# Input projections as seven block products in place of eight, with attention in 128-query chunks and a precomputed order

## The chip, the cores and the metric

The kernel runs on one core of a Trainium2 chip. The metric is the time of one execution on the device in microseconds (us); the kernel before takes 602.11 us, the median of three runs.

## What is computed

Causal attention over 2 batches, 12 heads, 448 positions and 64 dimensions, and then two two-layer networks on its 896 x 768 result, one behind the other, all in float32:

```
scores = q @ k.T / 8, masked above the diagonal; attn = softmax(scores)
x = (attn @ v), heads side by side                          # 896 x 768
h = x @ w_in;  g = h * clip(h + 3, 0, 6) / 6;  x = g @ w_out    # 768 -> 2048 -> 768
h = x @ w_in2; g = max(h, 0) + alpha * min(h, 0); y = g @ w_out2
```

## The kernel before

Activations are kept transposed, features on the 128 partitions and tokens along the row. 448 tokens are one block, so there are two blocks (`blk`, halves of the positions of both batches), 6 tiles of input features (`KIN`) and 16 tiles of hidden features (`KFF`). A projection is done in a split form: each float32 operand is written as a high and a low part of a reduced type (`split`, L80 on ScalarE for the high part, L81 on VectorE for the low one), and `three` (L233 to L235) multiplies high by high, high by low and low by high. Weights come as raw 64-bit words, whose conversion to float32 takes two ScalarE and two VectorE instructions of 768 columns (L207, L209, L210, L213) ahead of their split.

Attention (L89 to L180) goes over 6 pairs of heads and 2 blocks of queries, both batches each: scores (L123), a reduction on VectorE that adds the mask and finds the row maximum (L128), an exponential on ScalarE (L132), the division on GpSimd (L141), transposes on TensorE (L152) with copies out of PSUM, and the weighting of v (L165). Chunks are of 112 queries. The two heads of a pair lie on different halves of the partitions.

The input projection (`unit`, L254) forms one hidden tile of one block with 6 x 3 matmuls, applies the activation (`act1`, `act2`) and splits the result. The output projection (`outputs`, L266) forms one output tile of both blocks over all 16 hidden tiles, with weights in pieces of 5, 5 and 6 tiles. The weights' loads and conversions run some pieces ahead (`Pieces.get`). The order on each engine comes from the scheduler of the language, which sets it by a simulated time line; loads go through the queue of the Sync engine (SP), stores through ScalarE's.

Of the kernel before, what the change touches and what calls it, by code (L numbers as in the profile page):

```python
# [18 lines left out]
P = 128  # L19
CH = 112  # L20
NCH = S // CH
HALF = 2 * CH
NT = B * HALF
NBLK = 2
KIN = DM // P
KFF = DFF // P
BANK = 512
CUTS = ((0, 5), (5, 10), (10, 16))
LAST = 12
MASK = -1.0e9 * D ** 0.5  # L30
SCALE = 1.0 / D ** 0.5


def f32(t):
    return t.bitcast(F32)


class Job:


    def __init__(self, blk, c):
        self.blk, self.c = blk, c
        self.nk = 2 * (blk + 1)
        self.rows = [(i, (2 * blk + i + 1) * CH) for i in range(2)]
        self.off = [0, self.rows[0][1]]

        if blk == 0:
            self.groups = [[(0, 0, 0), (1, 1, 2 * CH)]]
        else:
            self.groups = [[(0, 0, 0), (1, 0, 2 * CH)], [(2, 0, 0), (3, 1, 2 * CH)]]  # L50


@with_exitstack
def fused_kernel(ctx: ExitStack, tc: tile.TileContext, q, k, v, w1i, w1o, w2i, w2o, alpha, out):
    nc = tc.nc
    psum = bass.MemoryType.PSUM

    const = ctx.enter_context(tc.tile_pool(name="const", bufs=1))
    xp = ctx.enter_context(tc.tile_pool(name="x", bufs=1))
    wp = ctx.enter_context(tc.tile_pool(name="w", bufs=3))  # L60
    hp = ctx.enter_context(tc.tile_pool(name="h", bufs=1))
    ps_m = ctx.enter_context(tc.tile_pool(name="ps_m", bufs=1, space=psum))

    ident = const.tile([CH, CH], F32, name="ident")
    mask = const.tile([CH, S], F32, name="mask")
    alpha_sb = const.tile([P, KFF], F32, name="alpha_sb")

    def diagonal(t, op, fill):
        nc.gpsimd.affine_select(
            out=t, in_=t, compare_op=op, fill=fill, base=0, pattern=[[-1, CH]], channel_multiplier=1  # L70
        )

    nc.gpsimd.memset(mask, 0.0)
    nc.gpsimd.memset(ident, 0.0)
    diagonal(mask[:, S - CH:S], ALU.is_ge, MASK)
    diagonal(ident, ALU.not_equal, 1.0)

    def split(hi, lo, src):

        nc.scalar.copy(hi, src)  # L80
        nc.vector.tensor_sub(lo, src, f32(hi))  # L81

    xs = {}

    def split_x(src, blk, c):
        xh = xp.tile([P, NT], F32R, tag=f"xh{blk}{c}", name="xh")
        xl = xp.tile([P, NT], F32R, tag=f"xl{blk}{c}", name="xl")
        split(xh, xl, src)
        xs[blk, c] = (xh, xl)  # L89

    def load(j):
        j.q = att.tile([P, B, HALF], F32, tag="q", name="q")
        nc.sync.dma_start(out=j.q, in_=q[j.c, :, :, j.blk * HALF:(j.blk + 1) * HALF])  # L96
        j.k = att.tile([P, B, j.nk * CH], F32, tag="k", name="k")
        nc.sync.dma_start(out=j.k, in_=k[j.c, :, :, 0:j.nk * CH])  # L98
        j.v = att.tile([CH, 2, B, j.nk, D], F32, tag="v", name="v")
        for b in range(B):  # L100
            nc.sync.dma_start(out=j.v[:, :, b], in_=v[:, 2 * j.c:2 * j.c + 2, b, 0:j.nk, :])  # L101

    def scores(j, b):
        cols = j.off[1] + j.rows[1][1]
        j.e[b] = [att.tile([CH, cols], F32, tag="e", name="e", bufs=8) for _ in range(2)]
        j.nm[b] = att.tile([CH, 2, 2], F32, tag="nm", name="nm")
        j.sm[b] = att.tile([CH, 2, 2], F32, tag="sm", name="sm")
        s = {}
        for i, n in j.rows:
            w = slice(i * CH, (i + 1) * CH)  # L110
            for side in range(2):
                if j.blk == 0 and i:
# [192 lines left out]
    n = 0  # L305
# [45 lines left out]
```

## Time and profile before

| | |
|---|---|
| runs | 600.57, 602.11, 604.17 us |
| profiled execution, span from first to last instruction | 601.3 us |
| TensorE (PE) busy | 582.3 us, 97% |
| VectorE (DVE) busy | 333.8 us, 56% |
| ScalarE (ACT) busy | 331.9 us, 55% |
| GpSimd (POOL) busy | 48.3 us, 8% |
| mean granted TensorE clock | 0.983 |

The profile is of one execution. Its span is the distance from the first to the last instruction, and the execution's own time is known only through the runs: the span stands between the fastest and the median run. Busy time of TensorE is taken from modelled ends of pipelined matmuls, so the distance from one start to the next says more than the length of a row. A fp32 matmul of attention appears as two rows. [...] A row of the time line gives start, length, engine, line, operation, output and inputs, and in brackets the idle time ahead of it with what ended it.

### The profile page before, as it was taken

What the parts mean: (1) busy time and instruction counts of PE and PEld (TensorE: products, weight loads), DVE (VectorE), ACT (ScalarE), POOL (GpSimd) and SP (SyncE); (2) the same over time, 40 slices, a digit from 0 to 9 for tenths busy, and PEclk for the clock granted to TensorE, in tenths of its full rate; (3) what the DMA queues carried; (4) which work ended last, traced back from release to release, by engine and by line L of the source; (5) the groups of instructions that cost most, each with busy time, mean ns of one, the idle gap of its engine ahead of it and who ended that gap; (6) DMA issues with size and microseconds to landing.
All of it is one profiled execution on the core that took longest, in us unless ns stands there. A gap on an engine that the chain in (4) does not pass through costs nothing.

```text
span 601.3 us, 8117 instructions
## 1 busy us (share of the span) xinstructions
PE 582.3 (97%) x3024; PEld 496.5 (83%) x3024; DVE 333.8 (56%) x632; ACT 331.9 (55%) x629; POOL 48.3 (8%) x104
## 2 busy tenths in 40 slices
PE   5799999889999999999999999999999999999997
PEld 2355555469999999999999999999999999999996
DVE  3566665855777755754444454777776654344310
ACT  4566775845755655643443445887777754334210
POOL 2334445030000000000000000000000000000000
PEclk9889999789999999999999999999999999999999
DMA  8523334413333322343323433333323333453000
GB/s 235 168 64 88 114 93 136 158 53 105 106 106 105 102 93 87 100 137 121 116 88 106 158 106 105 106 106 105 106 87 100 128 105 119 126 156 112 32 32 31
DMA packets 23224, 64.63 MB, mean 108 GB/s; under 512 B 2192, under 2 KB 13712, under 8 KB 23184
## 3 DMA queue, kind: packets, MB, share of 16 engines
q1 hardware_dynamic: 21456, 61.36, 32.5%
q10 hardware_dynamic: 1728, 2.75, 1.2%
q8 instruction: 24, 0.39, 0.3%
q14 instruction: 16, 0.13, 0.1%
HBM read 61.35 MB, written 2.75 MB: 107 GB/s over the span
## 4 chain that ended last, share of the span: by engine, by line
PE 93%; DMA 3%; SPq 1%; ACT 1%; DVE 1%; issue 0%; ACTq 0%
PE m L234 26%; PE m L233 26%; PE m L235 26%; PE o L165 6%; PE t L152 5%; PE s L123 4%; DMA raw<-w1i 2%; DMA k<-k_t 1%; SPq L101 0%; DVE raw L210 0%; ACT wf L207 0%; SPq L96 0%; SPq L98 0%; ACT raw L209 0%; DVE e L128 0%
## 5 line engine op out<-in xcount | busy, mean ns | idle before, releaser
L233 PE MATMUL m<-xh,hi 128*128 128x448 f32 x384 | 141.5, 368 | 2.7 <-ACT xh L80 2.7
L234 PE MATMUL m<-xl,hi 128*128 128x448 f32 x384 | 140.9, 367 | 0.0
L233 PE MATMUL m<-gh,hi 128*128 128x448 f32 x384 | 140.2, 365 | 0.0
L235 PE MATMUL m<-gh,lo 128*128 128x448 f32 x384 | 140.2, 365 | 0.0
L234 PE MATMUL m<-gl,hi 128*128 128x448 f32 x384 | 140.2, 365 | 0.0
L235 PE MATMUL m<-xh,lo 128*128 128x448 f32 x384 | 140.2, 365 | 0.0
L81 DVE TENSOR_TENSOR lo<-wf,hi 128x768 fp32r<-128x768 f32 (+1 forms) x68 | 61.9, 911 | 96.2 <-ACT hi L80 95.2
L80 ACT CAST hi<-wf 128x768 fp32r<-128x768 f32 (+1 forms) x68 | 54.2, 797 | 89.9 <-PE m L234 89.8
L210 DVE SCALAR_TENSOR_TENSOR raw<-wf,raw 128x768 uint32<-128x768 uint32 (+1 forms) x68 | 62.1, 913 | 67.7 <-ACT wf L207 58.0
L233 PEld LDWEIGHTS m<-xh,hi 128*128 128x128 f32 x384 | 72.3, 188 | 10.0 <-ACT xh L80 2.9
L234 PEld LDWEIGHTS m<-xl,hi 128*128 128x128 f32 x384 | 72.1, 188 | 7.0 <-issue 1.0
L209 ACT ACTIVATE raw<-raw 128x768 uint32<-128x768 uint32 (+1 forms) x68 | 59.3, 873 | 32.9 <-DMA raw<-w1o 13.2
L235 PEld LDWEIGHTS m<-gh,lo 128*128 128x128 f32 x384 | 72.1, 188 | 5.7
L233 PEld LDWEIGHTS m<-gh,hi 128*128 128x128 f32 x384 | 72.1, 188 | 5.7
L234 PEld LDWEIGHTS m<-gl,hi 128*128 128x128 f32 x384 | 72.1, 188 | 5.7
L235 PEld LDWEIGHTS m<-xh,lo 128*128 128x128 f32 x384 | 72.1, 188 | 5.6
L207 ACT ACTIVATE wf<-raw 128x768 f32<-128x768 f32 (+1 forms) x68 | 57.9, 851 | 30.4 <-DVE lo L81 22.4
L213 DVE SCALAR_TENSOR_TENSOR wf<-wf,raw 128x768 uint32<-128x768 uint32 (+1 forms) x68 | 61.8, 909 | 1.5
L132 ACT ACTIVATE e<-e,nm 112x112 f32<-112x112 f32 (+2 forms) x96 | 50.0, 523 | 20.5 <-DVE nm L128 16.1
L80 ACT CAST gh<-hg 128x448 fp32r<-128x448 f32 x64 | 36.0, 562 | 38.3 <-DVE hg L243 21.7
L141 POOL TENSOR_SCALAR e<-e,r 112x112 f32<-112x112 f32 (+1 forms) x96 | 47.0, 507 | 78.9 <-DVE r L137 64.2
L123 PE MATMUL s<-k,q 64*112 64x112 f32 (+3 forms) x192 | 42.9, 500 | 10.7 <-DMA k<-k_t 4.9
(32 smaller groups left out, 425.8 us busy)
## 6 DMA issues: line engine op xcount, KB each, us to landing
raw<-w1i SPq DMA_DIRECT2D x16, 768.0 KB, 4.4
raw<-w2i SPq DMA_DIRECT2D x16, 768.0 KB, 4.2
raw<-w1o SPq DMA_DIRECT2D x12, 640.0 KB, 4.0
raw<-w2o SPq DMA_DIRECT2D x12, 640.0 KB, 4.1
raw<-w1o SPq DMA_DIRECT2D x6, 768.0 KB, 4.3
raw<-w2o SPq DMA_DIRECT2D x6, 768.0 KB, 4.3
q<-q_t SPq DMA_DIRECT2D x12, 224.0 KB, 3.5
k<-k_t SPq DMA_DIRECT2D x6, 448.0 KB, 3.7
```

The lines of the kernel that those rows point to most:

```text
L80: nc.scalar.copy(hi, src)
L81: nc.vector.tensor_sub(lo, src, f32(hi))
L123: nc.tensor.matmul(s[i, side], lhsT=j.q[d, b, w], rhs=j.k[d, b, 0:n], start=True, stop=True)
L132: nc.scalar.activation(e, e, AF.Exp, bias=nm, scale=-1.0, accum_out=sm)
L141: nc.gpsimd.tensor_scalar(e, e, r[:, side, i:i + 1], 1.0, ALU.mult, ALU.mult)
L207: nc.scalar.activation(f32(w), f32(high), AF.Copy, scale=2.0 ** -112)
L209: nc.scalar.activation(low, low, AF.Copy, bias=-0.4999, scale=2.0 ** -29 * (1 - 2.0 ** -16))
L210: nc.vector.scalar_tensor_tensor(out=low, in0=w, scalar=3, in1=low, op0=ALU.logical_shift_left, op1=ALU.bitwise_or)
L213: nc.vector.scalar_tensor_tensor(out=w, in0=w, scalar=0x80000000, in1=low, op0=ALU.bitwise_and, op1=ALU.bitwise_or)
L233: nc.tensor.matmul(ps, lhsT=hi[:, w], rhs=xh, start=start, stop=False)
L234: nc.tensor.matmul(ps, lhsT=hi[:, w], rhs=xl, start=False, stop=False)
L235: nc.tensor.matmul(ps, lhsT=lo[:, w], rhs=xh, start=False, stop=stop)
```

## The change

**Input projection.** Strassen's scheme replaces the plain product. Hidden tiles m and m + 8 form a pair, the input features are cut in two halves of three tiles, and the tokens are the two blocks, each now one batch: a 2 x 2 by 2 x 2 product of blocks with seven products (`w_in`, named by b11, t1, t2, b22, t3, b21, t4) in place of eight. Each product is 3 tiles x 3 matmuls. The sums of x (t1 to t4) are formed and split once per tile in `take_x`; the sums of the weights (s12, s34) are formed on VectorE for every pair, and all three 768-column sets and one of 384 columns are split. PSUM banks a and c keep running sums: they are read between two products (`kept`), and the next product adds to the same bank (`again=not start`). What is read is added up in SBUF tiles on VectorE (`add_to`), then the activation follows (`finish`).

**Output projection.** Three output tiles of both blocks at a time (six banks), in two passes over the hidden tiles. The high and low parts of the hidden tiles are made in the first pass.

**Attention.** Twelve units (head pair, batch) with query chunks of 128, 128, 128 and 64; in the last chunk both heads share one matmul of 128 rows. Transposed blocks are packed into four banks per unit. Keys and queries of a unit come in one load.

**Order.** A program written in the kernel (`Plan.solve`) puts every instruction on its engine at build time, from costs given with it, due times and numbers of buffers. Stores go through SP's queue.

The core of the diff:

```diff
...
-    def three(ps, hi, lo, i, xh, xl, start, stop):
-        w = slice(i * P, (i + 1) * P)
-        nc.tensor.matmul(ps, lhsT=hi[:, w], rhs=xh, start=start, stop=False)
-        nc.tensor.matmul(ps, lhsT=hi[:, w], rhs=xl, start=False, stop=False)
-        nc.tensor.matmul(ps, lhsT=lo[:, w], rhs=xh, start=False, stop=stop)
...
-    def unit(pool, layer, blk, m, hi, lo):
-
-        ps = pool.tile([P, NT], F32, tag="m", name="m")
-        for kk in range(KIN):
-            three(ps, hi, lo, kk, *xs[blk, kk], kk == 0, kk == KIN - 1)
-        g = act2(ps, m) if layer else act1(ps)
-        gpool = gp["first"] if (blk, m) == (0, 0) else gp["last"] if m >= LAST else gp["main"]
-        gh = gpool.tile([P, NT], F32R, tag=f"gh{blk}_{m}", name="gh")
-        gl = gpool.tile([P, NT], F32R, tag=f"gl{blk}_{m}", name="gl")
-        split(gh, gl, g)
-        gs[blk, m] = (gh, gl)
-
-    def outputs(pool, n, done):
-
-        for c in range(KIN):
-            tiles = [pool.tile([P, NT], F32, tag="m", name="m") for _ in range(NBLK)]
-            for k0, k1 in CUTS:
-                hi, lo = pieces.get(n)
-                n += 1
-                for blk in range(NBLK):
-                    for kk in range(k0, k1):
-                        three(tiles[blk], hi, lo, kk - k0, *gs[blk, kk], kk == 0, kk == KFF - 1)
-                    if k1 == KFF:
-                        done(tiles[blk], blk, c)
-        return n
...
+                    if ok:
+                        key = (round(t, 2), o.due, o.index)
+                        if best is None or key < best[0]:
+                            best = (key, e, o, t)
...
+        return sorted(done, key=lambda o: (o.start, o.index))
...
+    def take_x(self, layer, c, blk, ps):
+
+        j, low = c % HK, c < HK
+        x, f = self.x, self.f
+        src, n = (lambda: ps.tile[:, 0:S]), f"{layer}{j}"
+
+        def parts(which, t):
+            x[layer, which, j] = self.split("u", which + n, S, lambda: t.tile, t)
+
+        if low and blk:
+            f["b12", j] = Buf("u", "b12" + n, S, F32)
+            self.copy(f["b12", j], src, ps, S)
+        elif low:
+            x[layer, "b11", j] = self.split("u", "b11" + n, S, src, ps)
+            b12 = f["b12", j]
+            f["t1", j] = self.combine("t1" + n, lambda: b12.tile, src, b12, ps)
+            parts("t1", f["t1", j])
+        elif blk:
+            x[layer, "b22", j] = self.split("u", "b22" + n, S, src, ps)
+            b12, t1 = f["b12", j], f["t1", j]
+            f["t2", j] = self.combine("t2" + n, src, lambda: t1.tile, ps, t1)
+            t3 = self.combine("t3" + n, src, lambda: b12.tile, ps, b12)
+            parts("t2", f["t2", j])
+            parts("t3", t3)
...
+            x[layer, "b21", j] = self.split("u", "b21" + n, S, src, ps)
+            t2 = f["t2", j]
+            parts("t4", self.combine("t4" + n, src, lambda: t2.tile, ps, t2))
...
+    def three(self, ps, hi, lo, at, x, start, stop, due, again=False):
+
+        nc, (xh, xl) = self.nc, x
+
+        def emit(_):
+            w, out = slice(at, at + P), ps.tile[:, 0:S]
+            for lhs, rhs in ((hi, xh), (hi, xl), (lo, xh)):
+                nc.tensor.matmul(
+                    out, lhsT=lhs.tile[:, w], rhs=rhs.tile, start=start and lhs is hi and rhs is xh,
+                    stop=stop and lhs is lo, skip_group_check=again)
+
+        self.cols += 1
+        return self.plan.op((PE, 0.605), emit, reads=[hi, lo, xh, xl], writes=[ps], due=due + self.cols * 0.605, chain="moe")
...
+    def w_in(self, layer, m, src, due):
+        nc, op = self.nc, self.plan.op
+        w1, w2 = self.convert(src[m]), self.convert(src[m + PAIRS])
+        s12, s34 = Buf("w", "s12", DM, F32), Buf("w", "s34", DM, F32)
...
+        add, sub = nc.vector.tensor_add, nc.vector.tensor_sub
+        sums(s12, right, w2, left, w2, right, add, [w2])
+        sums(s12, left, s12, right, w1, left, sub, [(s12, W3), w1])
+        sums(s34, right, w1, right, s12, left, sub, [w1, (s12, 0)])
+        sums(s34, left, w1, left, w2, left, sub, [w1, w2])
...
+        p12 = both("a1", DM, lambda: f32(w1.tile), [w1])
+        p56 = both("s12", DM, lambda: s12.tile, [(s12, 0), (s12, W3)])
+        p37 = both("s34", DM, lambda: s34.tile, [(s34, 0), (s34, W3)])
+        p4 = both("a2", W3, lambda: f32(w2.tile[:, right]), [w2])
...
+        def product(ps, parts, at, which, start):
+            for kk in range(HK):
+                o = self.three(ps, *parts, at + kk * P, self.x[layer, which, kk], start and kk == 0,
+                               kk == HK - 1, due, again=not start)
+            return o.due
...
+        product(a, p12, 0, "b11", True)
+        g11 = kept("g11", a)
+        product(c, p56, W3, "t1", True)
+        g22 = kept("g22", c)
+        product(a, p56, 0, "t2", False)
+        g12 = kept("g12", a)
+        end = product(c, p37, W3, "b22", False)
+        add_to(g12, c)
+        finish(g12, m, 1, end + 5.0)
+        end = product(a, p37, 0, "t3", False)
+        add_to(g22, a)
+        finish(g22, m + PAIRS, 1, end + 5.0)
+        end = product(b, p12, W3, "b21", True)
+        add_to(g11, b)
+        finish(g11, m, 0, end + 5.0)
+        end = product(a, p4, 0, "t4", False)
+        g21 = Buf("u", "g21", S, F32)
+        finish(g21, m + PAIRS, 0, end + 4.0, ps=a)
+
+    def w_out(self, layer, src, due, done):
+        halves = {}
+        for h in range(2):
+            banks = {(j, blk): Buf("ps", f"y{j}{blk}") for j in range(HK) for blk in range(2)}
+            for k0 in range(0, PAIRS, 2):
+                parts = []
+                for kp in (k0, k0 + 1):
+                    w = self.convert(src[h, kp])
+                    parts.append(self.split("w", "wo", DM, lambda w=w: f32(w.tile), w))
+                order = [(j, blk) for j in range(HK) for blk in (1, 0)]
+                if h == 0 and k0 == 0:
+                    order = [(j, blk) for blk in (1, 0) for j in range(HK)]
+                for j, blk in order:
+                    for i, kp in enumerate((k0, k0 + 1)):
+                        for kk, k in enumerate((kp, kp + PAIRS)):
+                            if h == 0 and (k, blk) not in halves:
+                                g = self.g[k, blk]
+                                halves[k, blk] = self.split("u", f"g{k}{blk}", S, lambda g=g: g.tile, g)
+                            o = self.three(banks[j, blk], *parts[i], kk * W3 + j * P, halves[k, blk], k == 0,
+                                           k0 == PAIRS - 2 and i == 1 and kk == 1, due)
+                    if k0 == PAIRS - 2:
+                        done(layer + 1, HK * h + j, blk, banks[j, blk])
...
+    def build(self):
+        nc, op, d = self.nc, self.plan.op, self.dram
+        start, step = 9.0, 6.2
+        for n in range(2 * KIN):
+            self.attend(n, n // 2, 1 - n % 2, start + (n + 1) * step)
...
+        due = start + 2 * KIN * step - 2.0
+        for layer, (w_in, w_out) in enumerate((("w1i", "w1o"), ("w2i", "w2o"))):
+            for m in range(PAIRS):
+                self.w_in(layer, m, d[w_in], due)
+            self.w_out(layer, d[w_out], due, self.take_x if layer == 0 else self.store)
...
+SLOTS = {"u": 50, "w": 14, "raw": 3, "kq": 2, "v": 3, "e": 12, "el": 3, "small": 6, "a": 2, "ps": 8, "alpha": 1}
...
+            o.emit(o.eng)
...
```

How the order of the instructions stands on the engines, at three places. VectorE, one hidden tile of both blocks in layer 0 before (L243 activation, L81 low parts, L210 and L213 conversion):

```order
L243 SCALAR_TENSOR_TENSOR hg<-hr,m 128x448
L81 TENSOR_TENSOR gl<-hg,gh 128x448
L210 SCALAR_TENSOR_TENSOR raw<-wf,raw 128x768
L243 SCALAR_TENSOR_TENSOR hg<-hr,m 128x448
L213 SCALAR_TENSOR_TENSOR wf<-wf,raw 128x768
L210 SCALAR_TENSOR_TENSOR raw<-wf,raw 128x768
L81 TENSOR_TENSOR gl<-hg,gh 128x448
```

Each activation is followed by the low part of its result, with the conversion of later weights between them. VectorE in the changed kernel, part of one pair of hidden tiles in layer 0 (L209 and L212 conversion, L418 sums of weights, L430 their low parts, L457 additions out of PSUM, L466 activation):

```order
L212 SCALAR_TENSOR_TENSOR wf<-wf,raw 128x768
L418 TENSOR_TENSOR s_1491<-wf 128x384
L430 TENSOR_TENSOR a1l<-wf,a1h 128x768
L418 TENSOR_TENSOR s_1491<-s_1491,wf 128x384
L457 TENSOR_TENSOR g_1489<-c,g_1489 128x448
L418 TENSOR_TENSOR s_1513<-wf,s_1491 128x384
L430 TENSOR_TENSOR s12l<-s_1491,s12h 128x768
L457 TENSOR_TENSOR g_1471<-a,g_1471 128x448
L466 SCALAR_TENSOR_TENSOR g_1489<-r,g_1489 128x448
```

The sums of weights and the additions out of PSUM are new, and the low parts of the hidden tiles no longer stand there.

TensorE in the changed kernel, where the second unit's weighting ends and the third and fourth units' scores begin (L387 weighting, L297 the last chunk's scores, L291 those of the others):

```order
L387 MATMUL o<-a,v 64x448 x2
L387 MATMUL o<-a,v 64x320 x2
L297 MATMUL sl<-kq 128x448
L387 MATMUL o<-a,v 64x192 x2
L291 MATMUL s_293<-kq 128x384
L291 MATMUL s_294<-kq 128x384
L387 MATMUL o<-a,v 64x64 x2
L291 MATMUL s_303<-kq 128x256
L291 MATMUL s_304<-kq 128x256
```

The scores of two units now stand together, ahead of the transposes of the first of them; before, the scores of part of a unit alternated with transposes and weighting.

## Rows read from the trace of the kernel before

**Rows 1.** The page's first part: busy time, share of the span, instructions.

```profile
span 601.3 us, 8117 instructions
PE 582.3 (97%) x3024; PEld 496.5 (83%) x3024; DVE 333.8 (56%) x632; ACT 331.9 (55%) x629; POOL 48.3 (8%) x104
```

**Rows 2.** Busy time by stretch of the span; the first line names the columns.

```profile
core 0: us, PE busy (x) PEld busy (x) DVE busy (x) ACT busy (x) POOL busy (x), PEclk, DMA share, GB/s
...
20.00:39.62 19.62, 15.74 (x80) 8.56 (x78) 11.93 (x44) 12.82 (x39) 6.11 (x14) 0.74 0.22 69
39.62:57.04 17.42, 17.42 (x126) 9.92 (x125) 12.42 (x51) 12.32 (x41) 7.02 (x16) 1.00 0.37 107
...
109.30:133.40 24.10, 22.25 (x141) 13.57 (x141) 17.55 (x39) 14.88 (x35) 5.51 (x8) 0.85 0.31 99
133.40:597.80 464.40, 464.36 (x2296) 429.90 (x2292) 253.19 (x331) 247.71 (x375) 0.00 (x0) 1.00 0.32 103
```

**Rows 3.** Time line of TensorE, end of the last output projection: 54 steps apart.

```profile
586.04 0.36 PE L233 MATMUL m<-gh,hi 128*128 128x448 f32 x1
...
596.98 0.37 PE L233 MATMUL m<-gh,hi 128*128 128x448 f32 x1
```

**Rows 4.** Time line of all engines behind the last matmul.

```profile
597.39 0.37 PE L235 MATMUL m<-gh,lo 128*128 128x448 f32 x1
597.80 0.53 ACT L282 COPY o<-m 128x448 f32<-128x448 f32 x1 [3.12 <-PE m L235]
598.36 0.34 ACTq L283 DMA_DIRECT2D y_t<-o  x1
```

**Rows 5.** Time line of VectorE in attention, 70 to 72 us.

```profile
70.00 0.50 DVE L128 CUSTOM_DVE_ANT_0 e<-s,mask 112x336 f32<-112x336 f32 x1
...
70.42 0.62 DVE L128 CUSTOM_DVE_ANT_0 e<-s,mask 112x448 f32<-112x448 f32 x1
...
70.96 0.62 DVE L81 TENSOR_TENSOR xl<-o,xh 128x448 fp32r<-128x448 f32 x1
71.50 0.49 DVE L128 CUSTOM_DVE_ANT_0 e<-s,mask 112x336 f32<-112x336 f32 x1
```

**Rows 6.** Time line of VectorE in the first input projection.

```profile
150.51 0.96 DVE L210 SCALAR_TENSOR_TENSOR raw<-wf,raw 128x768 uint32<-128x768 uint32 x1 [2.23 <-ACT wf L207]
...
151.51 0.96 DVE L213 SCALAR_TENSOR_TENSOR wf<-wf,raw 128x768 uint32<-128x768 uint32 x1
...
152.39 0.62 DVE L81 TENSOR_TENSOR gl<-hg,gh 128x448 fp32r<-128x448 f32 x1
```

**Rows 7.** Groups by line and shape, ScalarE: busy us, mean ns of one.

```profile
L209 ACT ACTIVATE raw<-raw 128x768 uint32<-128x768 uint32 x44 | 40.3, 916 | 18.5 <-DMA raw<-w2i 5.5 <-DMA raw<-w1i 5.3 <-DMA raw<-w1o 4.5
...
L242 ACT ACTIVATE hr<-m 128x448 f32<-128x448 f32 x32 | 17.2, 539 | 7.4 <-PE m L235 7.4
```

**Rows 8.** Time line of TensorE in attention, 56 to 75 us.

```profile
56.98 1.01 PE L123 MATMUL s<-k,q 64*112 64x448 f32 x4
57.92 0.59 PE L152 MATMUL t<-ident,e 112*112 112x112 f32 x4
58.44 0.59 PE L165 MATMUL o<-a,v 112*64 112x224 f32 x2
...
72.31 1.55 PE L165 MATMUL o<-a,v 112*64 112x224 f32 x16
73.79 0.47 PE L234 MATMUL m<-xl,hi 128*128 128x448 f32 x1
```

**Rows 9.** Time line of ScalarE in attention.

```profile
58.69 0.67 ACT L132 ACTIVATE e<-e,nm 112x448 f32<-112x448 f32 x1 [1.42 <-DVE nm L128]
...
59.35 0.85 ACT L154 COPY a<-t 112x448 f32<-112x448 f32 x2
...
65.99 0.38 ACT L132 ACTIVATE e<-e,nm 112x112 f32<-112x112 f32 x1
...
66.36 0.47 ACT L132 ACTIVATE e<-e,nm 112x224 f32<-112x224 f32 x1
```

**Rows 10.** Time line of TensorE, its first matmuls.

```profile
4.89 2.59 PE L123 MATMUL s<-k,q 64*112 64x112 f32 x16 [4.89 <-DMA k<-k_t]
```

**Rows 11.** Waits of the whole span: total us, times, longest.

```profile
DVE lo L81 <- ACT hi L80: 95.2, 50, 6.6
```

More of the change, by code (lines that the diff above doesn't have):

```diff
@@ L7 @@
 from concourse import mybir
-from concourse.bass import opposite_side
 from concourse._compat import with_exitstack
@@ L35, in f32, with __init__ @@
     return t.bitcast(F32)
[L38 to L48, printed above, removed]
-        else:
-            self.groups = [[(0, 0, 0), (1, 0, 2 * CH)], [(2, 0, 0), (3, 1, 2 * CH)]]
+class Buf:
+    def __init__(self, cls, name, cols=None, dtype=None):
+        self.cls, self.name, self.cols, self.dtype = cls, name, cols, dtype
+        self.left, self.end, self.slot, self.tile = 0, 0.0, None, None
@@ L68, in diagonal @@
     def diagonal(t, op, fill):
         nc.gpsimd.affine_select(
[L70 to L89, printed above, removed]
@@ L94, in load @@
[L94 to L112, printed above, removed]
-                    s[i, side] = bank[side][:, j.off[1]:j.off[1] + n]
-                else:
-                    t = ps_s.tile([CH, BANK], F32, tag="s", name="s")
-                    s[i, side] = t[:, 0:n]
-                    if side == 0:
-                        bank = [t]
-                    else:
-                        bank.append(t)
-            for side in range(2):
-                d = slice(side * D, (side + 1) * D)
-                nc.tensor.matmul(s[i, side], lhsT=j.q[d, b, w], rhs=j.k[d, b, 0:n], start=True, stop=True)
-        for i, n in j.rows:
-            for side in range(2):
-                e = j.e[b][side][:, j.off[i]:j.off[i] + n]
-                nm, sm = j.nm[b][:, side, i:i + 1], j.sm[b][:, side, i:i + 1]
-                nc.vector.tensor_tensor_reduce(
-                    out=e, in0=s[i, side], in1=mask[:, S - n:S], scale=-SCALE, scalar=3.0e38,
-                    op0=ALU.add, op1=ALU.min, accum_out=nm,
-                )
-                nc.scalar.activation(e, e, AF.Exp, bias=nm, scale=-1.0, accum_out=sm)
@@ L304, in fused_kernel @@
-    gp["last"] = ctx.enter_context(tc.tile_pool(name="g_last", bufs=1, reuse_waits="tile"))
-    n = 0
-    for layer, done in enumerate((split_x, store)):
-        for m in range(KFF):
-            if layer or m:
-                parts = pieces.get(n)
-                for blk in range(NBLK):
-                    unit(ps, layer, blk, m, *parts)
-            n += 1
-        n = outputs(ps, n, done)
+            out=t, in_=t, compare_op=op, fill=fill, base=0, pattern=[[-1, P]], channel_multiplier=1)
@@ L320 @@
     c = np.ascontiguousarray
[L321 to L339 removed]
+    cuts = ((3 * P, S), (2 * P, 3 * P), (P, 2 * P), (0, P))
@@ new lines @@
+    y = r.results[0]["y_t"].reshape(DM, B, S)
+    out = np.empty((B, S, DM), np.float32)
+    at = 0
+    for lo, hi in cuts:
+        out[:, lo:hi] = y[:, :, at:at + hi - lo].transpose(1, 2, 0)
+        at += hi - lo
+    return out.reshape(B * S, DM)
```

542 lines of the change are left out of this document (384 added, 158 removed), and 4 rows, old and new, of the table banks.

## The prediction

> **What bounds the kernel now.** I read the page's busy times first, then the table of stretches, then the matmul rows at the end, and last the attention rows of each engine. TensorE is busy 97% of the span, VectorE 56%, ScalarE 55% [rows 1]. The table of stretches splits the span in two [rows 2]. [...] Before 133.4 us the kernel computes attention, and there all engines matter: in a steady period of 17.42 us (one of the six head pairs) TensorE is shown busy throughout, VectorE 12.42 us, ScalarE 12.32 us. At the end of the span matmuls start every 0.2026 us: from 586.04 to 596.98 us lie 54 steps [rows 3]. So the 2304 projection matmuls cost 2304 x 0.2026 = 466.8 us. The last ends near 597.75 us, which leaves 130.9 us ahead of or between them, and 3.5 us of copy and store behind [rows 4]. The sum is made against the profiled span of 601.3 us; the median of the runs is 602.1, 0.8 above it, and I add that at the end.
>
> **Projection matmuls.** Per pair of hidden blocks the input projection has 7 products of 9 matmuls, 63, where it had 72. Sixteen pairs save 144 of 2304; 2160 are left, as the changed order's rows also count. At 0.2026 us that is 29.2 us off, if nothing else becomes late. Of the 2160, 24 stand among the attention rows, so 2136 x 0.2026 = 432.8 us remain behind it. The output projection keeps its 1152 matmuls; the order of accumulation alone changes.
>
> **What Strassen puts on VectorE.** A VectorE step is the distance from one start to the next where nothing waits. A 336-column reduction takes 0.42 us, a 448-column one 0.54, a 448-column subtraction 0.54 [rows 5]. A 768-column step is 0.88 us where the next instruction does not read its result (L213 to the gl row), and 1.00 where it does (L210 to L213) [rows 6]. The new 384-column sums have no row: between 0.42 and 0.54, I take 0.47, the value on the line through 448 and 768 columns. Per pair: four bit operations 4 x 0.88 = 3.5; four sums 1.9; three low parts of 768 and one of 384 columns 3.1; three additions out of PSUM and four activations 7 x 0.54 = 3.8. That is 12.3 us; 13 of the 48 PSUM copies stand on VectorE, 0.15 more, and one or two steps per pair read the row before them, 0.12 each. About 12.6 us against TensorE's 63 x 0.2026 = 12.76: VectorE goes from 55% to 99% of TensorE's time in this stage. The cover is gone, so anything that makes VectorE late now reaches TensorE. With 15 pairs behind the attention I allow 4 us, between 0 and 8. ScalarE has at most 4 bit operations, 3.5 splits, 4 activations and 2.2 copies, under 10.5 us even at 0.92 for each 768-column one and 0.54 for each of 448 [rows 7], and stays out of it. The splits of the 32 hidden tiles of each layer are moved behind the last pair, among the output matmuls: the rows from pair 7's last activation to pair 8's hold 90 us of VectorE work beside 192 x 0.608 + 12.8 = 129 us of matmuls, so they cost nothing; without that cover they would add 32 x 0.54 = 17 us a layer. At the seam of the layers I put 1 us.
>
> **Attention.** A fp32 matmul is here two rows in the trace, and the two sides of a head pair run side by side. The 448-column pair takes 0.94 us from 56.98 to 57.92, four transposes 0.52 us, and the weighting of 784 columns (both sides together) 1.48 us from 72.31 to 73.79 [rows 8]. That is 0.0021 us a score column, 0.13 a transpose of 112 (0.149 for 128 columns in proportion), 0.0019 a weighting column. Old, per period: 2240 score columns 4.7, 40 transposes 5.2, 2240 weighting columns 4.2, 3 projection matmuls 0.6: 14.7 of 17.42 us, so 84% is work and the rest hand-offs. New, per unit (head pair, batch): 128 + 256 + 384 + 448 = 1216 score columns 2.55, 16 transposes 2.38, 448 + 320 + 192 + 64 = 1024 weighting columns 1.93: 6.86 us. Twelve units are 82.3, with the 24 projection matmuls 87.2 us. Of the transposes 36 write two 64-column pieces; no row shows such a store. Between no change and twice the price it is 0 to 5 us; I take 0, the price of the transposes that do have rows. VectorE's rows up to TensorE's last weighting come to 78 us: 84 reductions at 0.08 + 0.00103 per column, 31; 23 copies of 512 columns at 0.61, 14; 27 splits and combinations of x, 14.5; the first weights, 14; the rest 4. ScalarE has about 77: an exponential of 448 columns steps 0.66 us and one of 112 columns 0.37 [rows 9], so 84 take 44, copies 12, splits and weights 21. GpSimd's 40 us are hidden as before. TensorE first ran at 4.89 us, released by a load [rows 10]; the new first load, 480 KB by the code, is about as large as the q and k that it replaces, so 4.9 stands. The stage then ends no earlier than 4.9 + 87.2 = 92 us (no hand-off ever waits), and 4.9 + 87.2/0.845 = 108 if the share of work stays as it was. I take 102, nearer 108, because three engines now have 77 to 87 us in the same stage, where VectorE and ScalarE had 71%; less than 108 because the old stage also lost time in 20 to 39.6 and in 109.3 to 133.4 us [rows 2], where weights were late, and the new order has their loads spread among the units'. 1 us is for the last splits of x.
>
> **Moved queues.** Stores go from ScalarE's queue to SP's, behind the weight loads; the last load is long done at the end, so the tail keeps its 3.5 us. Conversions of weights fall from 68 to 64.
>
> **Sum.** 102 + 1 + 432.8 + 4 + 1 + 3.5 = 544.3 us against 601.3: 29 us off from the matmuls, 28 from attention and its seam. With 0.8 for the median, 545.
>
> **Rivals.**
> *VectorE bounds the input projections.* If each of its 20 instructions per pair cost its whole duration (0.96 instead of 0.88, 0.62 instead of 0.54 [rows 5, 6]), a pair would take 12.3 + 20 x 0.08 = 13.9 us, 1.15 over TensorE; 15 pairs are 17 us in place of the 4: 558, up to 564 with a late attention. For it: VectorE already waits 95 us in all for ScalarE's high parts [rows 11], and each such wait is now paid. Against it: rows 5 and 6 show the next instruction starting 0.08 before the end of the last. [...]
> *The clock falls in attention.* [...] If the new stage, with VectorE and ScalarE as full as TensorE, ran at 0.80 throughout, TensorE's 87.2 us would become 109: 566.
> *Slower than before: the shared accumulator.* Banks a and c now hold sums that are read between two products and added to again. Four times per pair TensorE must not write on until the reader has finished, and only one other product, 9 x 0.2026 = 1.82 us, lies between. The read takes about 0.54, so a reader that starts more than 1.2 us after the product stops TensorE. With 64 such places, a mean stop of 0.9 us gives 58 us back: 602 and above. For it: the readers stand in the queue of a VectorE with 0.88 us steps ahead of them. Against it: ScalarE took 35 of the copies, and the last copy of the old kernel started at 597.80, about 0.05 us after its matmul [rows 4].
> *Attention packs tightly* and VectorE keeps up: 92 + 432.8 + 4.5 = 529 or less.
>
> **How the numbers follow.** The forecast (529 to 556) gets 0.70, VectorE as bound 0.13, the clock 0.08, the accumulator 0.04, less than 529 0.04; 0.01 is left for no change, since the order shows that the matmuls are in fact fewer. A difference of over 0.5% is what a measurement can tell. Range: 92 + 0.5 + 432.8 + 0 + 0.5 + 3.5 = 529 below; above, the VectorE case with attention ending at 108, 564. Faster 0.95, same 0.01, slower 0.04.
>
> **What would show it.** Right: about 2160 matmul rows of 448 columns starting every 0.2026 us; the last attention matmul near 102 us; VectorE over 90% busy in the input projections and TensorE still over 95%. Wrong: TensorE rows idle behind VectorE's low parts (the first rival), a granted clock under 0.9 before 100 us (the second), idle TensorE in front of products into a or c, released by a copy or an addition (the third), or an attention stage that ends outside 92 to 108 us.

## The result, and the profile after

The changed kernel takes **549.59 us** (median of 4 runs, 548.38 to 553.24) where the kernel before takes 603.14 (4 runs beside it): a ratio of 0.911, 95% interval 0.907 to 0.916. The profiled execution took 548.4 us with a span of 546.6; the forecast was 545 and a span of 544.3. The total is 0.8% off, but two groups of its terms are off by more, in opposite directions.

Busy time of the engines, from the page of the kernel after, to be read beside [rows 1]:

```profile
PE 528.2 (97%) x2712; PEld 459.8 (84%) x2712; DVE 428.0 (78%) x773; ACT 337.9 (62%) x627; POOL 53.5 (10%) x97
```

The table of stretches of the kernel after, beside [rows 2]: time, then busy time and instruction count of PE, PEld, DVE, ACT and POOL, TensorE's granted clock, DMA share, GB/s. The first line is the attention stage, the next two lie inside it, the fourth is the input projection of layer 0 behind the attention, the last that of layer 1.

```profile
4.20:109.34 105.14, 94.63 (x576) 58.86 (x576) 87.33 (x268) 81.07 (x230) 50.98 (x84) 0.94 0.38 132
26.10:40.00 13.90, 10.14 (x51) 6.59 (x51) 11.23 (x39) 11.09 (x35) 6.82 (x10) 0.75 0.39 132
60.00:80.00 20.00, 20.00 (x139) 11.69 (x138) 18.65 (x66) 16.73 (x53) 12.59 (x23) 1.00 0.38 115
109.34:206.00 96.66, 96.66 (x481) 89.60 (x478) 95.22 (x149) 71.56 (x115) 0.00 (x0) 1.00 0.33 115
322.00:425.00 103.00, 102.94 (x508) 94.76 (x507) 102.38 (x159) 75.38 (x121) 0.00 (x0) 1.00 0.35 121
```

In both input projections VectorE is busy 98 to 99% of the time, and TensorE hardly stops (102.94 of 103.00 us busy in layer 1). In the attention it is the other way round: TensorE is idle 105.14 - 94.63 = 10.5 us, all of it before 57 us, and from 26.10 to 40.00 us the granted clock falls to 0.75.

TensorE's time line at the seam, where the first projection matmul behind the attention follows the last weighting, and at the end of the span, with VectorE's last copy (beside [rows 3, 4]):

```profile
109.34 0.47 PE L404 MATMUL a<-t202h,s12h 128*128 128x448 f32 x1
...
542.62 0.36 PE L404 MATMUL y<-g150h,wol 128*128 128x448 f32 x1
543.01 0.62 DVE L230 COPY o<-y 128x448 f32<-128x448 f32 x1 [1.80 <-PE y L404]
```

From 109.34 to 543.01, where the last copy starts, lie 433.7 us; 2136 matmuls at 0.2026 are 432.8. The whole projection stage lost 0.9 us. The tail is 546.6 - 543.0 = 3.6 us.

VectorE's time line inside layer 0's input projection shows the steps that the forecast had to assume ([rows 5, 6]):

```profile
156.51 0.95 DVE L209 SCALAR_TENSOR_TENSOR raw<-wf,raw 128x768 uint32<-128x768 uint32 x1
157.38 0.62 DVE L466 SCALAR_TENSOR_TENSOR g<-g,a 128x448 f32<-128x448 f32 x1
157.91 0.62 DVE L230 COPY g<-a 128x448 f32<-128x448 f32 x1
...
160.18 0.55 DVE L430 TENSOR_TENSOR a2l<-wf,a2h 128x384 fp32r<-128x384 f32 x1
160.65 0.95 DVE L212 SCALAR_TENSOR_TENSOR wf<-wf,raw 128x768 uint32<-128x768 uint32 x1
```

A 768-column step is 0.87 us, a 448-column one 0.53, a 384-column one 0.47.

What is new stands in the attention. GpSimd's time line, three of twelve units (x6 joins the divisions of the first 384 query rows of both sides, two each of 384, 256 and 128 columns), and under it VectorE's over the second of these stretches:

```profile
12.60 2.75 POOL L338 TENSOR_SCALAR e<-e,small 128x384 f32<-128x384 f32 x6
...
38.92 5.35 POOL L338 TENSOR_SCALAR e<-e,small 128x384 f32<-128x384 f32 x6
...
79.94 2.75 POOL L338 TENSOR_SCALAR e<-e,small 128x384 f32<-128x384 f32 x6
```

```profile
39.42 0.95 DVE L430 TENSOR_TENSOR s12l<-s,s12h 128x768 fp32r<-128x768 f32 x1
40.28 0.62 DVE L222 TENSOR_TENSOR t100l<-t,t100h 128x448 fp32r<-128x448 f32 x1
40.82 0.62 DVE L318 CUSTOM_DVE_ANT_0 el<-sl,mask 128x448 f32<-128x448 f32 x1
41.36 0.08 DVE L318 DVE_READ_ACCUMULATOR2_ANT small<- 128x1 f32 x1
41.36 1.17 DVE L430 TENSOR_TENSOR s34l<-s,s34h 128x768 fp32r<-128x768 f32 x1
...
42.99 1.04 DVE L209 SCALAR_TENSOR_TENSOR raw<-wf,raw 128x768 uint32<-128x768 uint32 x1
```

The same six divisions take 2.75 us in some units and up to 5.35 in others. Meanwhile VectorE runs four instructions that read two SBUF tensors, and the two of 1.17 and 1.04 us are longer than their usual 0.95 us as well. TensorE's waits in the first 109 us (total, times, longest) name who is late:

```profile
PE t L353 <- POOL e L338: 4.9, 8, 1.2
PE t L345 <- POOL el L338: 1.4, 1, 1.4
PE a L404 <- DVE b1101l L222: 2.1, 1, 2.1
PE a L404 <- DVE b1100l L222: 2.1, 1, 2.1
```

PE's lines make up the 10.5 us of idle time: 6.3 behind divisions, and 4.2 behind something else. Among the attention stand the first matmuls of the projection; two of them stand in TensorE's order before the low part of x that they read is ready: VectorE made it only after reductions of later units. The first of the two, with the matmul before it:

```profile
29.68 0.47 PE L404 MATMUL a<-b1100h,a1h 128*128 128x448 f32 x1
32.26 0.55 PE L404 MATMUL a<-b1100l,a1h 128*128 128x448 f32 x1 [2.11 <-DVE b1100l L222]
```

### The profile page after: what moved, and what is told of

Its sections match the earlier page's. It is cut to its first block, busy times and chain, and to the rows that moved or that the text cites. A ratio compares the mean times of both kernels' runs of the same rounds, so it can differ in the third digit from the quotient of the medians.

```text
span 546.6 us, 7448 instructions
## 1 busy us (share of the span) xinstructions
PE 528.2 (97%) x2712; PEld 459.8 (84%) x2712; DVE 428.0 (78%) x773; ACT 337.9 (62%) x627; POOL 53.5 (10%) x97
## 3 DMA queue, kind: packets, MB, share of 16 engines
HBM read 59.38 MB, written 2.75 MB: 114 GB/s over the span
## 4 chain that ended last, share of the span: by engine, by line
PE 91%; DVE 3%; POOL 3%; ACT 1%; issue 1%; DMA 1%; POOLq 0%; DVEq 0%
PE y L404 42%; PE a L404 20%; PE c L404 10%; PE b L404 5%; PE o L387 5%; PE t L353 3%; PE s L291 3%; POOL e L338 3%; PE sl L297 2%; PE t L345 1%; DMA kq<-kq 1%; ACT e L323 1%; DVE e L318 1%; DVE t L239 0%; POOL el L338 0%
## 5 line engine op out<-in xcount | busy, mean ns | idle before, releaser
L207 ACT ACTIVATE raw<-raw 128x768 uint32<-128x768 uint32 x64 | 58.8, 919 | 40.6 <-DMA raw<-w2i 18.8
L205 ACT ACTIVATE wf<-raw 128x768 f32<-128x768 f32 x64 | 57.1, 903 | 16.1 <-PE y L404 13.5
L209 DVE SCALAR_TENSOR_TENSOR raw<-wf,raw 128x768 uint32<-128x768 uint32 x64 | 61.5, 962 | 2.6 <-ACT wf L205 2.6
L212 DVE SCALAR_TENSOR_TENSOR wf<-wf,raw 128x768 uint32<-128x768 uint32 x64 | 61.2, 957 | 1.5
L222 DVE TENSOR_TENSOR wol<-wf,woh 128x768 fp32r<-128x768 f32 x32 | 30.4, 953 | 21.4 <-PE y L404 17.3
L338 POOL TENSOR_SCALAR e<-e,small 128x384 f32<-128x384 f32 (+2 forms) x72 | 43.6, 628 | 0.0
L221 ACT CAST woh<-wf 128x768 fp32r<-128x768 f32 x32 | 26.3, 836 | 21.1 <-PE y L404 13.6
L323 ACT ACTIVATE e<-e,small 128x384 f32<-128x384 f32 (+2 forms) x72 | 35.7, 501 | 2.9 <-DVE small L318 2.7
L318 DVE CUSTOM_DVE_ANT_0 e<-s,mask 128x384 f32<-128x384 f32 (+2 forms) x72 | 26.7, 417 | 2.5 <-PE s L291 1.8
L387 PE MATMUL o<-a,v 128*64 128x448 f32 (+3 forms) x192 | 28.2, 401 | 0.0
L387 PEld LDWEIGHTS o<-a,v 128*64 128x64 f32 (+1 forms) x192 | 13.4, 137 | 17.3 <-issue 10.2
L430 DVE TENSOR_TENSOR s12l<-s,s12h 128x768 fp32r<-128x768 f32 x16 | 15.2, 951 | 12.4 <-PE y L404 12.4
L418 DVE TENSOR_TENSOR s<-wf 128x384 f32<-128x384 f32 x32 | 17.8, 555 | 8.3 <-PE y L404 7.7
L291 PE MATMUL s<-kq 64*128 64x384 f32 (+2 forms) x144 | 22.3, 426 | 0.0
L291 PEld LDWEIGHTS s<-kq 64*128 64x128 f32 x144 | 13.0, 197 | 9.9 <-issue 5.6
```

Source lines behind the costliest of these rows:

```text
L205: op((ACT, 0.85), lambda e: nc.scalar.activation(f32(w.tile), f32(words(1)), AF.Copy, scale=2.0 ** -112), reads=[(raw, "h")], writes=[w])
L207: op((ACT, 0.87), lambda e: nc.scalar.activation(words(0), words(0), AF.Copy, bias=-0.4999, scale=2.0 ** -29 * (1 - 2.0 ** -16)), writes=[ ...
L209: op((DVE, 0.87), lambda e: nc.vector.scalar_tensor_tensor(out=words(0), in0=w.tile, scalar=3, in1=words(0), op0=ALU.logical_shift_left, o ...
L212: op((DVE, 0.87), lambda e: nc.vector.scalar_tensor_tensor(out=w.tile, in0=w.tile, scalar=0x80000000, in1=words(0), op0=ALU.bitwise_and, o ...
L222: op((DVE, 0.14 + 0.00094 * cols), lambda e: nc.vector.tensor_sub(lo.tile, src(), f32(hi.tile)), reads=[key, hi], writes=[lo])
L291: nc.tensor.matmul(t.tile[:, off:off + (i + 1) * P], lhsT=kq.tile[rows, S + i * P:S + (i + 1) * P], rhs=kq.tile[rows, 0:(i + 1) * P], star ...
```

## Experiments

Experiments 1 to 4, 8 and 9 are one execution each. Experiment 4 leaves the attention as it is and ends it at 108.56 us against 109.34, so differences of under 1 us there say nothing.

**Theory:** attention ends 7.3 us later than forecast because the weights' new VectorE work holds GpSimd's divisions, and TensorE's transposes wait for them. **Rival:** TensorE's own rows and its lower clock set the end, and GpSimd is hidden. For the projections, the theory is that VectorE has almost nothing to spare; the rival is that its busy time overstates its load. The end of attention is read in each run as the start of the first projection matmul behind the last weighting (109.34 above).

**1. No divisions.** The seven GpSimd divisions of each unit emit nothing.

```diff
-            op((POOL, ...), lambda _, ...: nc.gpsimd.tensor_scalar(...),
+            op((POOL, ...), lambda _, ...: None,
```

> The 84 divisions on GpSimd (the softmax rows times the reciprocal of their sum, L338) are left out, so the attention output is not normalised; the order of every other instruction stays. Theory (divisions stand in the chain exponential - division - transpose, and 17 of them are lengthened while VectorE works on two SBUF inputs): the last weighting ends near 100 us instead of 109.3 and the span falls by 7 to 10 us, to about 538. Rival (TensorE's own rows and its lower clock before 40 us set the end of attention, GpSimd is hidden): the last weighting ends at 107 us or later and the span stays above 544.

Measured: span 540.5, end of attention 103.19.

```profile
3.91:103.13 99.22, 91.97 (x576) 58.98 (x576) 82.92 (x268) 80.31 (x230) 0.00 (x0) 0.95 0.42 140
```

The span falls 6.1 us, all of it in the attention: less than the theory's 7 to 10, but more than the rival allows. VectorE's busy time falls by 4.4 us too, with the same 268 instructions: it had been slowed by the divisions. TensorE is still idle 99.22 - 91.97 = 7.2 us, 4.1 of them before the two matmuls that wait for x's low parts. This run removes a whole step of the chain, so it does not yet show that the *meeting* costs the time.

**2. One input.** In the first two pairs of layer 0 each VectorE step on the weights that reads two SBUF tensors becomes one of the same columns on a single tensor.

```diff
+        def lone(out, src):
+            nc.vector.reduce_max(out.unsqueeze(2), src.unsqueeze(2), axis=mybir.AxisListType.X)
...
-            op((DVE, ...), lambda _: nc.vector.tensor_sub(lo.tile[:, 0:cols], src(), f32(hi.tile[:, 0:cols])),
+            op((DVE, ...), lambda _: lone(lo.tile[:, 0:cols], src()) if one else nc.vector.tensor_sub(...),
```

> In the first two pairs of layer 0 the bit operations, sums and low parts of the weights on VectorE (L209, L212, L418, L430) are replaced by instructions of the same columns that read one SBUF tensor only, so the products of these two pairs have other values; order and number of instructions stay. Theory (a GpSimd division is held while VectorE reads two SBUF tensors): the lengthened divisions before 80 us fall from 13 to about 4, their excess from 8.2 to under 2.5 us, and the last weighting ends 3 to 7 us earlier, near 104 us. Rival 1 (the long divisions are a symptom, GpSimd simply takes turns): as many lengthened divisions as before and no gain. Rival 2 (they are held, but nothing waits for them): the divisions get short and the last weighting still ends within 1 us of 109.3.

Measured: end of attention 102.64, 6.7 us earlier, with every division still there. GpSimd's groups (busy, mean ns), first of the kernel after, then of this run:

```profile
L338 POOL TENSOR_SCALAR e<-e,small 128x256 f32<-128x256 f32 x24 | 16.9, 717 | 0.0
L338 POOL TENSOR_SCALAR e<-e,small 128x384 f32<-128x384 f32 x24 | 16.9, 716 | 0.0
```

```profile
L341 POOL TENSOR_SCALAR e<-e,small 128x384 f32<-128x384 f32 x24 | 15.0, 637 | 0.0
L341 POOL TENSOR_SCALAR e<-e,small 128x256 f32<-128x256 f32 x24 | 12.3, 526 | 0.0
```

The 256-column divisions fall from 717 to 526 ns; after the change they had been as slow as those of 384 columns. The replacements last as long as what they replace (groups of 941 to 944 ns at 768 columns against 950 where the original meets no division), so VectorE's own load is the same and only the kind of its reads differs. The wait of TensorE's transposes for these divisions falls from 4.9 us to

```profile
PE t L356 <- POOL e L341: 1.2, 3, 0.7
```

while those for x's low parts stay (2.1 and 2.2 us). In the stretch from 26.10 to 40.00 TensorE now has

```profile
26.10:40.00 13.90, 11.56 (x69) 7.90 (x70) 12.92 (x43) 12.84 (x37) 6.93 (x14) 0.88 0.41 134
```

69 instructions instead of 51, at a clock of 0.88 instead of 0.75. The theory holds: both rivals fall. The clock rises as the waits shrink (over the attention from 0.94 to 0.97, TensorE's idle time from 10.5 to 6.9 us), although the edit is on VectorE alone. Not separated is whose delay counted: the edit frees the divisions, and it also takes 2.6 us of lengthening off VectorE (84.75 us busy for 87.33). The span falls by 3.4 us only, to 543.2: 0.9 us went in layer 1's input projection and 2.3 in its output projection, where from 366 us on the matmuls start 0.2067 us apart instead of 0.2026 (last section).

**3. Strassen undone.** 8 plain block products per pair; scheduler, attention and output passes kept.

```diff
-        a, b, c = Buf("ps", "a"), Buf("ps", "b"), Buf("ps", "c")
...
+        self.x[layer, c, blk] = self.split("u", f"x{layer}{c}{blk}", S, lambda: ps.tile[:, 0:S], ps)
```

> Strassen alone is undone: 8 block products of 9 matmuls per pair, no sums on VectorE, the same list scheduling, attention and output passes. Theory (the matmul count is what the stage costs, VectorE's additions cost it nothing there): 2304 matmuls at 0.2026 us, the projection stage 29 us longer than 434, 462 to 464 us; the attention stage ends 3 to 8 us earlier than 109.3 because VectorE and GpSimd no longer meet there; span 568 to 573. Rival (a part of the gain is the accumulation in place and the two output passes, or VectorE's work did cost TensorE time): the projection stage is under 458 us and the span under 565.

Measured: span 573.3. The attention stage and the stretch behind it:

```profile
4.13:104.30 100.17, 90.92 (x567) 55.69 (x567) 79.47 (x251) 80.52 (x224) 48.51 (x84) 0.95 0.48 162
104.30:215.00 110.70, 109.88 (x544) 101.51 (x541) 75.72 (x103) 64.43 (x102) 0.00 (x0) 1.00 0.32 107
```

Weighting ends 5.0 us earlier, as expected, and the projections stay at the pitch of 0.2026; the span is 0.3 us above what was expected. So Strassen is worth 573.3 - 546.6 = 26.7 us here: 144 matmuls, 29.2, and 1.8 for nine more matmuls that find room inside the attention (24 against 15), less the 5.0 us by which the weighting ends later with it; the 0.7 left over is a wait in this run, whose first projection matmul starts 0.85 us after the last weighting instead of 0.15. The expectation's reason for the 5.0, that VectorE and GpSimd no longer meet, is not borne out: GpSimd is busy 48.51 us for 50.98, and 10 divisions are still longer than others of their width, by 8.0 us in all (17 and about 10.5 us in the changed kernel), since the bit operations and low parts remain. What clearly falls is VectorE's work, 79.47 us for 87.33. The other 28.0 us of the change (601.3 to 573.3) came without Strassen, nearly all in the attention; what the larger chunks, the packed transposes and the new order each gave was not tried.

**4. One more low part.** 0.87 us more VectorE work in each of 14 pairs.

```diff
+            twice = name == "a1" and not (layer == 0 and m < 2)
...
+                for _ in range(1 + twice):
+                    nc.vector.tensor_sub(lo.tile[:, 0:cols], src(), f32(hi.tile[:, 0:cols]))
```

> In all pairs but the first two of layer 0 one 768-column low part (L430) is computed twice: 0.87 us more VectorE work per pair, 14 pairs, values unchanged. Theory (VectorE has 0.2 us of slack per pair of 12.76 us, 95.2 us busy of 96.7 in the first layer's pairs, so it is the next bound): TensorE waits 0.6 us per pair, 4 us in the first layer and 4 to 5 in the second, span 554 to 556. Rival (busy time overstates the load, or the weights prepared ahead cover it): the span grows by less than 2 us.

Measured: span 557.3. Layer 0's and layer 1's input projections:

```profile
108.50:210.30 101.80, 99.40 (x484) 89.62 (x481) 100.84 (x155) 71.23 (x116) 0.00 (x0) 1.00 0.32 109
327.20:436.60 109.40, 104.28 (x505) 93.82 (x504) 108.54 (x166) 74.59 (x121) 0.00 (x0) 1.00 0.33 109
```

From first to last matmul, layer 0 loses 4.65 us over 0.2026 a matmul (0.14 before) and layer 1 7.5 (0.5 before): 0.75 a pair in layer 0, where 0.12 was spare, and all 0.87 in layer 1. The theory was right and still too mild for layer 1, where no slack is left. Where TensorE then waits is of interest too, in layer 1:

```profile
PE a L404 <- DVE g L462: 5.1, 7, 1.3
```

L462 is the addition out of an accumulator that the next product needs.

**5 to 7. Buffers and order.** One kernel gets a third key-and-query buffer for one buffer of `u`; one gets the trace's costs and held divisions in the scheduler's model; one gets both.

```diff
-SLOTS = {"u": 50, ..., "kq": 2, ...}
+SLOTS = {"u": 49, ..., "kq": 3, ...}
```

```diff
-        op((PE, 0.24), score(0), ...)
+        op((PE, 0.42), score(0), ...)
...
+            if e == POOL:
+                if lock > t:
+                    o.out = o.end = clock[e] = o.end + lock - t
+                held = o
+            if e == DVE and o.two:
+                lock = o.end
+                if held is not None and held.end > t:
+                    held.out = held.end = clock[POOL] = held.end + o.end - t
```

> One more buffer for the scaled keys and queries of a unit (3 in place of 2), paid with one buffer of u; everything else is left to the scheduler with its old costs. Theory (TensorE idles before 40 us because the divisions of two units are late and it has no third unit's scores to compute meanwhile): the last weighting starts 3 to 7 us before 109.2 and the time falls by as much, to 543 to 547. Rival (the divisions and VectorE set the pace of the whole stage, however many units are open): within 1.5 us of 109.2.

> The same kernel, with the scheduler's costs of scores, weightings and ScalarE steps set to those of the trace, and a GpSimd division held in its model while VectorE has an instruction on two SBUF tensors; buffers unchanged. Theory (the order was made for divisions that are never held, so units whose division is late stand ahead of others in TensorE's queue): the excess of the divisions falls from 10.5 us to under 6 and the last weighting starts 2 to 5 us before 109.2. Rival (any order meets the same divisions, total work sets the end): within 1.5 us of it.

> Both: the trace's costs with the held divisions in the scheduler's model, and the third buffer of keys and queries. Theory: the gains add, the last weighting starts at 98 to 103 us and the time is 539 to 543. Rival (the two reach the same idle time): no better than the better of the two alone, within 1 us. In the projections nothing may move by over 2 us in either case, since TensorE runs there at 0.2026 us a matmul.

Measured against 602.95 us before (7 runs): third buffer **543.60** (ratio 0.902, 0.897 to 0.906), new costs **542.25** (0.901, 0.895 to 0.906), both **537.36** (0.894, 0.888 to 0.900; of its four runs three took 537.3 and one 543.39). The attention stages in this order:

```profile
4.15:101.55 97.40, 91.49 (x576) 55.98 (x576) 83.28 (x266) 78.29 (x227) 49.12 (x84) 0.98 0.41 137
```

```profile
4.20:106.40 102.20, 95.51 (x594) 62.69 (x594) 88.74 (x274) 84.19 (x237) 48.60 (x84) 0.98 0.41 136
```

```profile
4.00:97.15 93.15, 90.81 (x576) 59.41 (x576) 83.66 (x268) 80.02 (x231) 49.98 (x84) 1.00 0.44 150
```

The third buffer ends the stage 7.8 us earlier, a little more than expected; the new order 2.9 us, and it places 18 more matmuls (3.6 us) in the stage besides; the two together 12.1 us, more than expected. With both, TensorE is busy 90.81 of 93.15 us at full clock. But GpSimd is busy 49.12, 48.60 and 49.98 us, hardly less than the 50.98 of the change: the gain is not that divisions are held less, as the second expectation had it. The waits of TensorE tell more. Those for x's low parts, 4.2 us, are gone in all three, as the projection matmuls come later in its order. Those of the transposes for divisions were 4.9 us after the change; with the third buffer, and then with both, they are

```profile
PE t L353 <- POOL e L338: 5.0, 5, 1.8
PE t L366 <- POOL e L351: 0.3, 1, 0.3
```

So the third buffer alone leaves TensorE waiting for divisions as before. Only with the new order as well does TensorE have other units' work meanwhile. This version beats both kernels, and it is the one to keep.

**8. The same replacement in that kernel.** The diff of experiment 2, on the kernel with both.

> The replanned kernel with three key buffers, and in the first two pairs of layer 0 the VectorE steps on two SBUF tensors replaced by ones on a single tensor (the products of these pairs have other values); same order. Theory (what holds the last weighting at 97.1, 5 us over TensorE's own 92, is again mostly held divisions, whose excess is 9.2 us): the excess falls under 3 us and the last weighting starts at 93 to 95. Rival (with a third unit open TensorE has other work while a division is held): at 96.5 or later. The span then follows by at most as much, since VectorE has less than 0.2 us a pair to spare in the projections.

Measured: end of attention 96.09 against 97.21.

```profile
3.90:96.05 92.15, 89.61 (x576) 58.50 (x576) 81.93 (x268) 79.43 (x231) 42.63 (x84) 1.00 0.45 152
```

GpSimd's busy time falls by 7.35 us and the stage by 1.1: between the two expectations, nearer the rival. A held division costs little with a third unit open and the new order. The span rose to 541.4, which the last section explains.

**9. The meeting by itself.** Ahead of the attention GpSimd multiplies in a row while VectorE runs six blocks of ten.

```diff
+        for _ in range(60):
+            nc.gpsimd.tensor_scalar(gt, gt, gs, 1.0, ALU.mult, ALU.mult)
...
+        for f in (bank, one, both, bank, copy, both):
+            for _ in range(10):
+                f()
```

> The cost of the meeting by itself: ahead of the attention GpSimd multiplies a 256-column tile 60 times in a row, while VectorE, not waiting for it, runs six blocks of ten 448-column instructions: PSUM and SBUF in, one SBUF tensor in (the instruction of the run before), two SBUF tensors in, PSUM and SBUF again, a plain SBUF copy, two SBUF tensors again. Theory (GpSimd is held for the whole of each VectorE instruction that reads two SBUF tensors): GpSimd's instructions take 485 ns beside the first, second and fourth block, and over 1000 ns, or hardly any ends, beside the third and sixth; VectorE's own take up to 0.15 us longer where they meet. No theory for the copy. Rival (the two share bandwidth, no one is held): everything beside the third block is longer by the same modest share, under a third. The main part's time is not read from this run.

Measured, from the time line of GpSimd and VectorE around the second block, and then around the third:

```profile
9.45 6.76 POOL L595 TENSOR_SCALAR gt<-gt,gs 128x256 f32<-128x256 f32 x12
9.49 6.51 DVE L596 TENSOR_REDUCE zt<-xt 128x448 f32<-128x448 f32 x10
```

```profile
15.73 8.64 POOL L595 TENSOR_SCALAR gt<-gt,gs 128x256 f32<-128x256 f32 x11
16.03 8.00 DVE L598 TENSOR_TENSOR zt<-xt,yt 128x448 f32<-128x448 f32 x10
```

Of the third block, one instruction of each:

```profile
17.12 0.72 POOL L595 TENSOR_SCALAR gt<-gt,gs 128x256 f32<-128x256 f32 x1
17.53 0.78 DVE L598 TENSOR_TENSOR zt<-xt,yt 128x448 f32<-128x448 f32 x1
```

Beside one SBUF input GpSimd's instructions take 478 ns and start every 0.571 us; the blocks from PSUM and SBUF give the same. Beside two SBUF inputs both engines start one instruction every 0.816 us: GpSimd's take 723 ns, VectorE's 782 where alone they take 625. (These lengths and starts are those of single instructions; the rows of a whole block give only its sum.) Beside the plain copy GpSimd's take 490 ns, and the copies 549 (393 the first). Neither expectation met this: 51% longer is more than a modest share and less than being held for the whole. In a steady meeting the two alternate, one instruction each. The sharp holds of 0.7 us in the kernel, such as a 256-column division of 1.17 us at 41.71, are single divisions that met one 768-column instruction.

## Why the prediction was right, and where it was not

- **Matmuls.** "2136 x 0.2026 = 432.8": right. 2160 are left, 24 of them ahead of the last weighting, and the rest start at that pitch. Before, that stage was TensorE's alone, as the last line of [rows 2] shows, and TensorE still sets its pace.
- **Strassen's VectorE load.** "About 12.6 us against TensorE's 12.76": the steps were right (0.87, 0.53 and 0.47 us measured where the prediction took 0.88, 0.54 and 0.47), the sum was not. A pair has three copies out of PSUM, so the 13 of 48 that stand on VectorE are 0.44 us a pair and not 0.15; and more steps than assumed read the row before them. An estimate from the mean steps in the trace is 12.9 us a pair in layer 0 and 13.0 in layer 1, a little over TensorE's 12.76. TensorE does not stop because weights are prepared ahead, and the lead shrinks: one low part of each pair (s34l) is done 5.1 us before its first matmul in the second pair of layer 0 and 3.1 us in the eighth, 8.4 and 1.9 in layer 1.
- **"I allow 4 us"** for lateness in the input projections, 1 for the seam and 1 for x's splits: too much. Together they came to 0.9 us. Late steps did not add up, since the work done ahead covers them; where it no longer does (experiment 4) nearly all of the excess is paid.
- **Attention, "I take 102":** 109.3 measured, 7.3 us late and past the 108 that was meant as its upper bound; by the prediction's own sign this part was wrong. The 102 was 4.9 us of start, 87.2 of TensorE's work and 9.9 for hand-offs. Measured are 4.2, 90.8 (busy at full clock in experiment 7), and 14.3 for hand-offs: 10.5 of idle time and 3.8 by which TensorE's rows last longer at the clock of 0.94. So TensorE's term was 3.6 us short and the allowance 4.4. The step that failed is "GpSimd's 40 us are hidden as before". They became 51, with divisions held by VectorE, and TensorE waited 6.3 us for them; 4.2 more went to two matmuls ahead of their x, which the prediction did not think of. In the kernel before, VectorE's attention steps read PSUM, and one of its 96 divisions was longer than others of its width, by 0.9 us; the change puts two pairs' sums, low parts and bit operations among them. Experiment 2 gives 6.7 us back. That this is nearly the 7.3 is chance: TensorE's 3.6 us and the wait for x are still in it.
- **Tail.** 3.5 taken, 3.6 measured.
- **Sum.** 7.3 us too little in attention, 5.1 too much in the projections and their allowances (433.7 for 438.8), 0.1 too little in the tail: 546.6 for 544.3. The total was closer than its parts, and that was luck: the two errors have nothing to do with each other.
- **Rival, VectorE as bound:** did not come, because the next instruction starts 0.08 us before the last one's end, as [rows 5, 6] had shown, and because of the work done ahead; 0.87 against 0.95 us a step decides between no stall and 1.15 us a pair. Experiment 4 shows how near this rival was.
- **Rival, the clock:** in part. No run shows the 0.80 throughout that it took: the mean in attention was 0.94, and TensorE's busy time 94.63 us against 90.81 at full clock, so 3.8 us. The clock went with the waits: 0.94 with 10.5 us of idle TensorE, 0.97 with 6.9 in experiment 2, 1.00 with 2.3 in experiment 7.
- **Rival, the accumulators:** no stop of any size in the changed kernel; with VectorE 0.87 us slower a pair it is there that TensorE stops for the most part (5.1 of the 7.5 us in layer 1, experiment 4).

## What to carry over

When a change moves work onto an engine, look not only at its busy time but at what its instructions read, and at which other engine reads SBUF at the time: a helper engine that was hidden can come onto the path without one instruction more (here a 256-column division took 717 ns on average, and 526 with fewer such meetings). A stage in which one engine is full and another 98% full can run at the first one's floor, if work is prepared ahead (0.9 us lost in 433.7 here); test the margin by adding a little. A matmul that stands in the order before its operand is ready can leave its engine idle (2.1 us, twice here), so read every name in the list of waits and not only the expected one. When a chain cannot be made faster, one more buffer that gives the bound engine a third unit to work on, with an order made for it, may be worth more than shortening the chain.

## What was not expected of the hardware

**GpSimd and VectorE.** VectorE instructions on two SBUF tensors and GpSimd's lengthen each other. In a steady meeting GpSimd's took 723 ns for 478 and VectorE's 782 for 625 (experiment 9). There neither engine is held for a whole instruction of the other, since one of each takes 0.816 us, less than 0.478 + 0.625 = 1.10. Beside a reduction of one SBUF tensor, or a sum of one from PSUM and one from SBUF, GpSimd's stayed at 478, and beside a plain copy they took 490. With fewer meetings the 256-column divisions fell from 717 to 526 ns (experiment 2).

**Two pitches of TensorE.** 448-column matmuls in an unbroken row start every 0.2026 us in most runs, but in some stretches every 0.2067, at a granted clock of 1.00. The same stretch of layer 1's output projection, experiment 7 and then experiment 8:

```profile
440.00:520.00 80.00, 80.00 (x397) 74.13 (x396) 30.08 (x39) 19.45 (x25) 0.00 (x0) 1.00 0.24 82
```

```profile
440.00:520.00 80.00, 80.00 (x389) 72.67 (x388) 33.04 (x41) 21.87 (x27) 0.00 (x0) 1.00 0.27 87
```

In the same 80 us stand 397 matmuls of the one and 389 of the other. Experiment 8 runs so in the whole of its projections, 7.2 us more between the first and the last matmul; experiment 2 from 366 us to the end, 3.2 us more (578 matmuls in the 119.00 us from 420.00 on); the third-buffer kernel in the first output projection, 2.3 us (577 in the 119.00 us from 199.00 on). What sets the one or the other was not tried and stays open; a single span can be off by some us for it, and the four executions of the changed kernel lie within 4.9 us.
